# Band attention and a gated network: keys and queries of two heads stacked in the first batch, the global tokens last but one, due times set anew

## The chip, the cores and the metric

One core of a Trainium2 chip runs the whole program. The metric is device time in microseconds (us); the time before is 898.46 us, the median of three runs (897.37 to 899.85). Engine names: PE is the matrix engine (PEld its weight loads), DVE the vector engine, ACT the scalar engine, POOL the general engine, SP the engine whose queue issues every DMA here.

## What is computed

Eight batches of eight heads; 512 local and 32 global tokens a head, head size 64. A local token attends to the 32 global keys and to the local keys at most 32 positions away; a global token attends to all 544 keys. The outputs, 544 tokens of 8 x 64 = 512 values a batch, go through a network with a product gate.

```python
k_all = np.concatenate([k_g, k_l], axis=2)
s_g = scale * np.matmul(q_g, k_all.transpose(0, 1, 3, 2))          # global queries, all keys
s_ll = np.where(np.abs(pos[:, None] - pos[None, :]) <= 32, scale * q_l @ k_l.T, -1e9)
a_l = sm(np.concatenate([scale * q_l @ k_g.T, s_ll], axis=-1))     # local queries
attn = np.concatenate([sm(s_g) @ v_all, a_l @ v_all], axis=2)
h = (x @ w1) * (x @ w2) @ w3                                       # x: attn as 4352 rows of 512
return h @ w_out
```

## The kernel before

Every product is made of float32r parts: an operand is split in a high part (a cast, `hi_of`, mostly on ACT) and a low part (the difference, `lo_of`, on DVE or POOL), and the products of the parts are summed in PSUM.

**A head.** `load_k` brings the keys of one head twice, into the upper and the lower 64 partitions of `kr` (608 columns: local keys with the global ones copied between the blocks). `prep_k` splits them into `kh` and `kl`, `prep_q` puts the high part of the queries in partitions 0 to 63 of `qs` and the low part in 64 to 127. So one matmul over 128 rows multiplies both parts of the queries by `kh`, a second one by `kl`: `scores` issues 2 for each of 4 query blocks, 8 a head. Then follow the row maximum (`mmax`, DVE), the exponentials (`exps`, ACT), seven transposes (PE), the split of the transposed weights (`hi` and `lo`, seven pieces each, tiles PTh, PTl and G), the products with the values (`av`, PE), and a sum of two halves (`cb` on ACT, `sum` on DVE). Two heads make a pair: `join`, `mul` (normalize) and the split of the result into `x` (`xh`, `xl`).

**Global queries.** For each pair of heads `load_kp` brings the keys a second time, as 128 x 544 with one head in either half of the partitions; `prep_kp` splits them (`kph`, `kpl`), and `g_scores` multiplies them by `QG`, 4 matmuls of 272 columns.

**Weights.** In the first 130 us or so 32 packed pieces of the weights (512 KB each) are fetched and unpacked (`unit`: a shift and a merge on DVE, a scaling on ACT). Pieces w3 and wo are multiplied into one matrix (`fold`, 64 steps on PE, tile w34); pieces w12 are split into tiles `W12`, which the last stage uses. All `W12` tiles 0 to 3 are allocated at the start.

**The network.** A quarter of a block of 256 tokens is `first` (tiles ap, bp), a gate (`ga`, `gb`, `gh`, `gl`) and `second` (tile acc). 17 blocks: 16 of local tokens (two a batch) and one of the 256 global tokens of all batches, which comes last. `evict` and `store` write a block in two parts; local tokens go to 128 rows that follow each other (L600), global tokens to 4 places of 32 rows (L602).

**The order** is not the program's text but a list: `list_schedule` simulates five engines with the costs in `COST` and takes on each engine, among the steps whose inputs are there, the one whose due time is earliest. Due times are worked out from the head's number and shifted by the tables `DUE`, `HEADS`, `UNITS` and `SUMS`. `HOLD_A`, `HOLD_D` and `HOLD_H` (ns) are how long a step that two engines can do is kept from one of them: with `HOLD_D` DVE takes a step that POOL can do, with `HOLD_H` DVE takes the cast of a PSUM tile that ACT can do. `LATE` is a penalty in PE's choice.

Of the kernel before, what the change touches and what calls it, by code (L numbers as in the profile page):

```python
# [7 lines left out]
F32 = mybir.dt.float32  # L8
# [22 lines left out]
def i(ap):  # L31
# [12 lines left out]
    w12l=((691, 1300), (420, 752)), w34h=587, w34l=681, scores=897, transposes=690, values=560, gscores=505,  # L44
    gtrans=465, first=1440, second=1405, fold=900,
# [3 lines left out]
MARGIN, LATE, MAIN = 600, 6.0, 2.5e5  # L49
# [6 lines left out]
HOLD_A, HOLD_D, HOLD_P, HOLD_H = 0.1, 0, 90000, 2000  # L56
# [14 lines left out]
    av=(0, -8.3, -53.5, 0), cb=(0, -42.6, 22.6, 0), cg=(-24.3, 42.6, 2.5, 0), clear=(36.2, 0, 0, 0),  # L71
    eg=(11.2, -14.5, 60.9, 0), exps=(-77.6, 1.9, 61.5, 0), fetch=(-6.1, 67.6, -28.7, 0), first0=(0, 0, -0.5, 0),
    first1=(0, 0, 14.2, 0), fold=(0, 82.7, 0, 0), ga=(0, 0, 19.2, 0), gb=(0, 0, -4.6, 0), gh=(0, 0, -57.6, 0),
    gl=(0, 0, -25.9, 0), gw=(0, 35.2, 8.4, 0), hi0=(0, 9.7, -58.6, 0), hi1=(0, -25.8, -77.7, 0),
    hi2=(0, -54.5, -10.4, 0), hi3=(0, -77.2, -22, 0), hi4=(0, -21.9, 24.2, 0), hi5=(0, -3.2, -31.3, 0),
    hi6=(0, 14, 6.1, 0), inv=(-41, -86.6, -72.2, 0), invi=(-2.4, 7.2, -63.4, 0), invo=(-5.2, -59.2, 61.1, 0),
    join=(0, -72, 8.5, 0), joing=(0, 41.8, -10.6, 0), kh=(-29, -66.2, 23.9, 0), kl=(25, -37.7, 45.9, 0),
    kph=(-76.1, 18.5, 3.8, 0), kpl=(22.5, 58.7, 76.8, 0), lcs=(-13.6, 0, 0, 0), lk=(10.3, -26.8, -37.4, 0),
    lkp=(6.7, -0.4, 59.5, 0), lo0=(0, -27.3, -31.1, 0), lo1=(0, -41.7, -128.1, 0), lo2=(0, -80.3, -32.8, 0),
    lo3=(0, -22.1, -19.6, 0), lo4=(0, -11.9, 72.6, 0), lo5=(0, 15.6, 35.1, 0), lo6=(0, -109, -94.1, 0),  # L80
    lq=(9.1, -81.9, -50.8, 0), lqg=(34.3, 46.7, 4.5, 0), lv=(22.9, 41.7, 72.5, 0), lvg=(-24.1, 73.7, -106.8, 0),
    mg=(11.1, 4.8, 28.3, 0), mmax=(-67.6, -19.9, 10.3, 0), mul=(0, 2.8, -12.7, 0), ng=(-9.8, -40.4, 19.2, 0),
    out=(0, 0, 31.5, 0), qgh=(-9.8, 6, 147.2, 0), qgl=(36.9, -10.2, 1.5, 0), qh=(54.2, -4.8, 102.4, 0),
    ql=(-40, 112.7, 18.6, 0), s=(173.8, 31.8, -49.9, 0), second=(0, 0, -11.5, 0), sg=(-103.1, 12.4, -39.4, 0),
    store=(0, 0, 68.3, 0), sum=(0, -31.9, 18.7, 0), t=(0, -40.4, -94.3, 0), tg=(0, -106.1, 15.3, 0),
# [17 lines left out]
}  # L103
SUMS = (-30.2, -40.9, -14, 28.4, 21.4, -13.3, 36.6, 38.3)
# [81 lines left out]
def band_attention_glu_kernel(  # L186
# [120 lines left out]

    def prep_k(n, part, eng=None):
        if part == 0:
            T["kh", n] = p1.tile([128, KD], F32R, tag="kh", name=f"kh{n}")  # L310
            hi_of(T["kh", n], T["kr", n], eng)
        else:
            T["kl", n] = p1.tile([128, KD], F32R, tag="kl", name=f"kl{n}")
            lo_of(T["kl", n], T.pop(("kr", n)), T["kh", n], eng)

    def prep_q(n, part, eng=None):
        if part == 0:
            T["qs", n] = p1.tile([128, 512], F32R, tag="qs", name=f"qs{n}")
# [27 lines left out]
    def scores(n):  # L346
        qs, kh, kl = T.pop(("qs", n)), T.pop(("kh", n)), T.pop(("kl", n))
# [3 lines left out]
        T["sm", n] = p2.tile([128, 4], F32, tag="sm", name=f"sm{n}", bufs=4)  # L351
        for e in range(4):
# [124 lines left out]
    def g_scores(m):  # L477
        kph, kpl = T.pop(("kph", m)), T.pop(("kpl", m))
        sg = ps_1.tile([128, 2, 512], F32, tag="s", name=f"sg{m}")
        for j, kk in enumerate((kph, kpl)):  # L480
# [3 lines left out]
        T["sg", m] = sg  # L484
# [136 lines left out]
    def open_early():  # L621
        P["w12a"] = ctx.enter_context(tc.tile_pool(name="w12a", bufs=1))
        for m in range(MA):
            alloc_w12("w12a", m)
# [141 lines left out]
    def tile_orders():  # L766
        for k in (("k", 0), ("kp", 0), ("kp", 1), ("k", 1)):
            take("kr", NK, (*k, "r"), ("load", *k))
        for k in (("q", 0), ("q", 1), ("vg", 0)):
            take("qr", 3, (*k, "r"), ("load", *k))  # L770
# [4 lines left out]
        for n in range(NH):  # L775
            if n + 2 < NH:
# [22 lines left out]
    def head(n):  # L799
# [3 lines left out]
        add(("load", "k", n), dma(2), t - 12, (), load_k, n, nbytes=2 * 64 * KD * 4)  # L803
        add(("load", "q", n), dma(1), t - 12.1, (), load_q, n, nbytes=64 * 512 * 4)
        for c, tag, due, fn in (("k", "kr", t - 2.0, prep_k), ("q", "qr", t - 1.2, prep_q)):
            h, l = (c + "h", n), (c + "l", n)
            add(h, hi(COST[c + "h"], 600 if c == "k" else 512), due, [("load", c, n)], fn, n, 0, eng=True)
            add(l, either(c + "l"), due + 1.4, [h], fn, n, 1, eng=True)
            read(h, (c, n, "r"))
            read(l, (c, n, "r"), h)  # L810
            read(("s", n), h)
        read(("s", n), ("kl", n))
        add(("s", n), only("PE", COST["scores"]), t + 2.7, [("kl", n), ("ql", n)], scores, n)
# [76 lines left out]
    def global_pair(m):  # L890
# [3 lines left out]
        take("kph", 1, ("kph", m), ("kph", m))  # L894
        take("kpl", 1, ("kpl", m), ("kpl", m))
        add(("load", "kp", m), dma(1), t - 6.0, (), load_kp, m, nbytes=128 * S * 4)
        add(("kph", m), hi(COST["kph"], S), t + 2.3, [("load", "kp", m)], prep_kp, m, 0, eng=True)
        add(("kpl", m), either("kpl"), t + 4.0, [("kph", m)], prep_kp, m, 1, eng=True)
# [251 lines left out]
```

## Time and profile before

| | |
|---|---|
| median of the runs | 898.46 us |
| the profiled execution | 898.57 us, its span 896.8 us |
| PE busy | 844.0 us (94%), 6016 matmuls |
| DVE, ACT, POOL busy | 631.9, 631.4, 424.1 us |
| DMA | 87.06 MB, mean 97 GB/s |
| granted PE clock, mean | 0.983 of full speed |

A profile has a page with busy times, and views that can be cut to an engine, a line or a stretch of time: busy time by stretch, groups of instructions by line, waits (who waited for whom), instructions in order of time. The time above the span (1.8 us) is what lies around the first and the last instruction. The lines that the prediction reads are in a section below.

### The profile page before, as it was taken

The page shows a single profiled execution, that of the slowest core. Times are in us where ns is not written, and L with a number is a line of the kernel's source. Part 1 is how long each engine was busy: PE and PEld are TensorE (multiplying, and loading weights), DVE is VectorE, ACT ScalarE, POOL GpSimd, SP SyncE. Part 2 cuts the span into 40 slices and gives each one's busy share as a digit, 9 for nine tenths or more (in the row PEclk, how much of TensorE's full clock was granted, in tenths as well). Part 3 has the DMA queues.
Part 4 walks back from the last instruction along what each step waited for, and adds up shares of the span by engine and source line. Part 5 has one row for each costly group of instructions (what it writes and reads, how often), then busy time and mean ns, then how long its engine had stood idle before and what let it go on. Part 6 is the DMA issues. An engine that isn't in the chain of part 4 may idle for free.

```text
span 896.8 us, 17972 instructions
## 1 busy us (share of the span) xinstructions
PE 844.0 (94%) x6016; PEld 766.0 (85%) x6016; DVE 631.9 (70%) x1644; ACT 631.4 (70%) x1724; POOL 424.1 (47%) x492
## 2 busy tenths in 40 slices
PE   3879969799999999999999999999999999999995
PEld 2545549699899999999999999999999999999994
DVE  4998988778877778777777777777777787512111
ACT  5887887787878787878787878787877777512111
POOL 4454765655655555555555455555555545200000
PEclk9999989999999999999999999999999999999998
DMA  9877545332242423232323332323232311000000
GB/s 273 246 219 215 181 149 139 118 98 83 65 118 69 111 63 115 61 106 68 113 67 106 77 101 80 101 68 114 65 107 65 108 57 48 13 24 24 1 24 24
DMA packets 52853, 87.06 MB, mean 97 GB/s; under 512 B 16024, under 2 KB 17048, under 8 KB 52760
## 3 DMA queue, kind: packets, MB, share of 16 engines
q1 hardware_dynamic: 52760, 85.92, 33.1%
q8 instruction: 47, 0.77, 0.4%
q14 instruction: 46, 0.38, 0.2%
HBM read 76.84 MB, written 9.04 MB: 96 GB/s over the span
## 4 chain that ended last, share of the span: by engine, by line
PE 87%; DVE 4%; ACT 4%; DMA 2%; issue 1%; POOL 1%; SPq 1%; DVEq 0%; ACTq 0%; POOLq 0%
PE ap L555 7%; PE acc L585 7%; PE acc L587 7%; PE bp L555 7%; PE ap L556 7%; PE acc L586 7%; PE ap L557 7%; PE bp L556 7%; PE bp L557 7%; PE s L355 6%; PE av L446 6%; PE w L692 4%; PE t L391 3%; PE t L394 2%; PE av L441 2%; PE sg L482 2%
## 5 line engine op out<-in xcount | busy, mean ns | idle before, releaser
L555 PE MATMUL bp<-x,w12h 128*128 128x256 f32 x544 | 154.8, 285 | 0.8 <-DVE g__1696 L565 0.8
L555 PE MATMUL ap<-x,w12h 128*128 128x256 f32 x544 | 153.7, 283 | 0.0
L556 PE MATMUL ap<-x,w12h 128*128 128x256 f32 x544 | 152.1, 280 | 0.0
L557 PE MATMUL ap<-x,w12l 128*128 128x256 f32 x544 | 151.6, 279 | 0.0
L556 PE MATMUL bp<-x,w12h 128*128 128x256 f32 x544 | 151.2, 278 | 0.0
L557 PE MATMUL bp<-x,w12l 128*128 128x256 f32 x544 | 151.1, 278 | 0.0
L289 POOL TENSOR_TENSOR kl<-kr,kh 128x608 fp32r<-128x608 f32 x62 | 93.5, 1508 | 104.8 <-ACT kh L286 102.0
L363 ACT ACTIVATE P<-P,mn 128x192 f32<-128x192 f32 (+1 forms) x256 | 121.5, 477 | 5.5 <-DVE mn L359 4.8
L460 DVE TENSOR_TENSOR u<-av,cb 64x352 f32<-64x352 f32 x128 | 65.8, 521 | 58.5 <-ACT cb L286 55.8
L555 PEld LDWEIGHTS bp<-x,w12h 128*128 128x128 f32 x544 | 102.5, 188 | 1.9 <-DVE g__1696 L565 0.9
L556 PEld LDWEIGHTS ap<-x,w12h 128*128 128x128 f32 x544 | 103.6, 190 | 0.5
L555 PEld LDWEIGHTS ap<-x,w12h 128*128 128x128 f32 x544 | 103.5, 190 | 0.5
L556 PEld LDWEIGHTS bp<-x,w12h 128*128 128x128 f32 x544 | 102.5, 188 | 1.1
L557 PEld LDWEIGHTS ap<-x,w12l 128*128 128x128 f32 x544 | 103.4, 190 | 0.0
L557 PEld LDWEIGHTS bp<-x,w12l 128*128 128x128 f32 x544 | 102.4, 188 | 0.0
L359 DVE CUSTOM_DVE_ANT_0 P<-s,cs 128x192 f32<-128x192 f32 (+1 forms) x256 | 87.3, 387 | 7.7 <-PE s L355 5.6
L289 DVE TENSOR_TENSOR PTl<-t,PTh 32x96 fp32r<-32x96 f32 (+1 forms) x192 | 76.3, 397 | 19.2 <-ACT PTh L286 14.3
L286 ACT CAST PTh<-t 32x96 fp32r<-32x96 f32 (+1 forms) x190 | 66.5, 350 | 22.9 <-PE t L391 15.5
L286 ACT COPY cb<-av 64x352 f32<-64x352 f32 x128 | 57.0, 446 | 32.4 <-PE av L446 29.3
L355 PE MATMUL s<-kh,qs 128*128 128x192 f32 (+1 forms) x256 | 65.9, 292 | 8.5 <-DVE mg L497 3.3
L692 PE MATMUL w<-wo,w3f 128*128 128x512 f32 x128 | 63.8, 635 | 3.9 <-DVE wo L616 3.8
L446 PE MATMUL av<-PTl,vs 128*128 128x192 f32 (+1 forms) x256 | 64.5, 277 | 0.0
(786 smaller groups left out, 2350.8 us busy)
## 6 DMA issues: line engine op xcount, KB each, us to landing
kr<-in_kd_t_dram SPq DMA_DIRECT2D x128, 152.0 KB, 2.9
raw_w<-in_w_t_dram SPq DMA_DIRECT2D x24, 512.0 KB, 4.3
kpr<-in_kp_t_dram SPq DMA_DIRECT2D x32, 272.0 KB, 2.7
out_dram<-o SPq DMA_DIRECT2D x34, 256.0 KB, 2.2
qr<-in_q_t_dram SPq DMA_DIRECT2D x64, 128.0 KB, 2.7
vr<-in_v_t_dram SPq DMA_DIRECT2D x32, 256.0 KB, 2.7
R<-rd SPq DMA_DIRECT2D x64, 128.0 KB, 3.0
raw_wo<-in_wo_t_dram SPq DMA_DIRECT2D x8, 512.0 KB, 6.4
```

The lines of the kernel that those rows point to most:

```text
L286: (nc.scalar.copy if eng in (None, nc.scalar) else eng.tensor_copy)(dst, src)
L289: (eng or nc.gpsimd).tensor_sub(dst, src, f(hi))
L355: nc.tensor.matmul(st[:, e, 0:w], qs[:, 128 * e : 128 * e + 128], kk[:, o : o + w], start=(j == e % 2 == 0), stop=(j == 1), skip_group_che ...
L359: nc.vector.tensor_tensor_reduce(blk(n, e), T["st", n][:, e, 0 : WIN[e][1]], masks[e], -0.125, 3.0e38, ALU.add, ALU.min, T["mn", n][:, e : ...
L363: nc.scalar.activation(blk(n, e), blk(n, e), AF.Exp, bias=T["mn", n][:, e : e + 1], scale=-1.0, accum_out=T["sm", n][:, e : e + 1])
L446: nc.tensor.matmul(av[:, o : o + c1 - c0], v, pt[:, j, c0:c1], start=False, stop=(j % 2 == y == 1), skip_group_check=True)
L460: nc.vector.tensor_add(T["u", n // 2][r : r + 64, x], T.pop(("av", n, x))[r : r + 64, 0:352], T["cb", n][r : r + 64, x])
L555: nc.tensor.matmul(d, wh[:, k, c, :], x[:, 0, 0:w], start=(k == m % 2 == 0), stop=False, skip_group_check=True)
L556: nc.tensor.matmul(d, wh[:, k, c, :], x[:, 1, 0:w], start=False, stop=False, skip_group_check=True)
L557: nc.tensor.matmul(d, wl[:, k, c, :], x[:, 0, 0:w], start=False, stop=(k == 3), skip_group_check=True)
L585: nc.tensor.matmul(a, gh[:, m % 2, sl], wh, start=(m == 0), stop=False)
L692: nc.tensor.matmul(T["w34", t], T["w3f", t, j // 4][:, j % 4], T["wo"][:, j], start=(j == 0), stop=(j == 7))
```

## The change

In the first batch (heads 0 to 7) the keys of two heads are loaded once, one head in either half of the partitions, and split once; the same for the queries, whose tile `qs` is now 128 partitions with the high and the low part side by side. The four products of the parts can no longer be summed over 128 rows, so `scores` issues 16 matmuls of 64 rows a head instead of 8 of 128. The stacked keys are just what the global queries of the pair need, so for the first four pairs `load_kp` and `prep_kp` go, and `g_scores` reads pieces of `kh` and `kl`: 12 matmuls instead of 4, since the columns lie apart. Four of the stacked key tiles and all the stacked query tiles are placed in the memory of `W12` tiles 1 to 3 (names e..), which therefore can be filled only when the early scores are done (`free`).

The block of global tokens and the last local block change places (`kk`). All due times, `COST` of four entries and `LATE`, `HOLD_A`, `HOLD_D`, `HOLD_H` are new.

```diff
-    gtrans=465, first=1440, second=1405, fold=900,
+    gtrans=465, first=1395, second=1385, fold=900,
-MARGIN, LATE, MAIN = 600, 6.0, 2.5e5
+MARGIN, LATE, MAIN = 600, 3.0, 2.5e5
-HOLD_A, HOLD_D, HOLD_P, HOLD_H = 0.1, 0, 90000, 2000
+HOLD_A, HOLD_D, HOLD_P, HOLD_H = 400, 1500, 90000, 400
...
-    av=(0, -8.3, -53.5, 0), cb=(0, -42.6, 22.6, 0), cg=(-24.3, 42.6, 2.5, 0), clear=(36.2, 0, 0, 0),
+    av=(0, 2.3, 13.1, 0), cb=(0, -40.5, -5.7, 0), cg=(46.3, -55.7, -7.8, 0), clear=(26.7, 0, 0, 0),
...
     def load_k(n):
-        nc.sync.dma_start(kr[0:64], kd_t[b, h])
-        nc.sync.dma_start(kr[64:128], kd_t[b, h])
+        if n < H:
+            nc.sync.dma_start(kr, kd_t[b, h : h + 2].rearrange("h d k -> (h d) k"))
+        else:
+            nc.sync.dma_start(kr[0:64], kd_t[b, h])
+            nc.sync.dma_start(kr[64:128], kd_t[b, h])
...
+    def early_tile(tag):
+
+        return P["w12a"].tile([128, 4, 2, 128], F32R, tag=f"w12{tag}", name=f"e{tag}_").rearrange("p a b c -> p (a b c)")
+
...
-            for j, kk in enumerate((kh, kl)):
-                nc.tensor.matmul(st[:, e, 0:w], qs[:, 128 * e : 128 * e + 128], kk[:, o : o + w],
-                                 start=(j == e % 2 == 0), stop=(j == 1), skip_group_check=True)
+            c = slice(128 * e, 128 * e + 128)
+            for j in range(4 if n < H else 2):
+                q, k = (qs[r : r + 64, j // 2, c], ks[j % 2][r : r + 64]) if n < H else (qs[:, c], ks[j])
+                nc.tensor.matmul(st[:, e, 0:w], q, k[:, o : o + w], start=(j == e % 2 == 0),
+                                 stop=(j == (3 if n < H else 1)), skip_group_check=True)
...
+        if m < NP:
+
+            for j, kk in enumerate((T["kh", 2 * m], T["kl", 2 * m])):
+                for e, c, o, w in ((0, 0, 0, 128), (0, 128, 160, 128), (0, 256, 320, 16),
+                                   (1, 0, 336, 112), (1, 112, 480, 128), (1, 240, 128, 32)):
+                    nc.tensor.matmul(sg[:, e, c : c + w], QG[:, m], kk[:, o : o + w], start=(j == c == 0), stop=(j == 1),
+                                     skip_group_check=True)
+            return
...
-        key, w = (divmod(k, 2), 256) if k < 2 * B else ((B, 0), TG)
+
+        kk = {2 * B: 2 * B - 1, 2 * B - 1: 2 * B}.get(k, k)
+        key, w = (divmod(kk, 2), 256) if kk < 2 * B else ((B, 0), TG)
...
+            if kind == "w12":
+                free = {1: [("s", 2), ("s", 3), ("sg", 1)], 2: [("s", n) for n in range(H)],
+                        3: [("s", 6), ("s", 7), ("sg", 3)]}.get(a, [])
```

What it moves, at the places that matter below. The first operations of ACT, before (kr, qr, kpr are keys, queries and pair keys as loaded, numbered by head or pair; raw_ are packed weights):

```order
L286 CAST QG_79<-qgr0_107 64x4x32
L286 CAST kh0_147<-kr0_112 128x608
L286 CAST kph0_155<-kpr0_116 128x544
L614 ACTIVATE raw_wo0_0_121<-raw_wo0_0_121 128x512
L286 CAST kph1_176<-kpr1_118 128x544
L489 COPY cg0_179<-sg0_166 64x2x272
```

and now (eh1 is the key tile of heads 2 and 3, eh2 and el2 the query tiles of the first two pairs):

```order
L294 CAST QG_79<-qgr0_93 64x4x32 x2
L294 CAST kh0_118<-kr0_95 128x608
L294 CAST eh1__127<-kr2_98 128x608
L294 CAST eh2__154<-qr0_102 128x512
L519 COPY cg0_158<-sg0_137 64x2x272
L644 ACTIVATE raw_w30_0_104<-raw_w30_0_104 128x512
L294 CAST el2__191<-qr2_107 128x512
```

The casts of pair keys are gone, and a key or query cast serves two heads. The scores of head 0 on PE, before:

```order
L692 MATMUL w34_0_185<-wo_95,w3f0_0_135 128x512
L355 MATMUL s0_194<-kh0_147,qs0_139 128x192
L355 MATMUL s0_194<-kl0_157,qs0_139 128x192
L355 MATMUL s0_194<-kh0_147,qs0_139 128x256
L355 MATMUL s0_194<-kl0_157,qs0_139 128x256
```

and now, the last global piece ahead of them:

```order
L508 MATMUL sg0_137<-kl0_123,QG_79 128x32
L378 MATMUL s0_170<-kh0_118,eh2__154 128x192
L378 MATMUL s0_170<-kl0_123,eh2__154 128x192
L378 MATMUL s0_170<-kh0_118,eh2__154 128x192
L378 MATMUL s0_170<-kl0_123,eh2__154 128x192
L378 MATMUL s0_170<-kh0_118,eh2__154 128x256
L378 MATMUL s0_170<-kl0_123,eh2__154 128x256
```

Each block of columns is met four times instead of twice, and two global scores run ahead of the first fold. The end of SP's queue, before:

```order
L600 DMA out_0_dram<-o7_0_128_11295 128x512
L600 DMA out_0_dram<-o7_1_0_11581 128x512
L600 DMA out_0_dram<-o7_1_128_11583 128x512
L602 DMA out_0_dram<-o8_0_0_11802 4x32x512
L602 DMA out_0_dram<-o8_0_128_11804 4x32x512
```

and now:

```order
L630 DMA out_0_dram<-o7_0_128_11300 128x512
L632 DMA out_0_dram<-o8_0_0_11601 4x32x512
L632 DMA out_0_dram<-o8_0_128_11603 4x32x512
L630 DMA out_0_dram<-o7_1_0_11822 128x512
L630 DMA out_0_dram<-o7_1_128_11824 128x512
```

The stores of the global tokens (o8) are no longer the last.

## Rows read from the trace of the kernel before

**Rows 1.** Busy time by stretch: from:to, length, engines (instructions), PE clock, DMA share, GB/s.

```profile
0.00:20.00 20.00, 5.89 (x16) 3.96 (x17) 8.22 (x20) 10.01 (x21) 10.18 (x15) 1.00 0.90 272
20.00:120.00 100.00, 88.64 (x356) 51.81 (x354) 90.11 (x221) 82.09 (x219) 54.16 (x66) 0.97 0.73 215
120.00:185.00 65.00, 48.95 (x325) 45.75 (x326) 53.28 (x135) 50.22 (x140) 42.64 (x51) 0.87 0.40 120
185.00:250.00 65.00, 63.59 (x490) 60.54 (x490) 51.33 (x134) 51.70 (x146) 35.89 (x42) 1.00 0.32 95
250.00:780.00 530.00, 530.00 (x4072) 504.75 (x4070) 407.25 (x1103) 417.34 (x1167) 276.10 (x313) 1.00 0.30 83
```

**Rows 2.** Waits of PE, 0 to 190 us: total us, times, longest.

```profile
PE sg L482 <- ACT kph L286: 10.9, 1, 10.9
PE tg L516 <- DVE mn L359: 6.6, 1, 6.6
```

**Rows 3.** The last stores: wait, issues; landing of ordinary stores; two stretches as in Rows 1.

```profile
SPq L1146 <- DMA out_dram<-o: 7.4, 1, 7.4
886.99 1.34 SPq L602 DMA_DIRECT2D out_dram<-o  x2
DMA to landing us min/median/max: 2.0/2.0/2.1
860.00:861.00 1.00, 1.00 (x11) 1.00 (x10) 0.22 (x1) 0.00 (x0) 0.00 (x0) 1.00 0.88 336
892.00:893.00 1.00, 0.00 (x0) 0.00 (x0) 0.00 (x0) 0.00 (x0) 0.00 (x0) 0.50 0.26 100
```

**Rows 4.** PE in order of time: start, us of the record, instruction.

```profile
75.21 0.28 PE L355 MATMUL s<-kh,qs 128*128 128x192 f32 x1
...
76.13 7.05 PE L692 MATMUL w<-wo,w3f 128*128 128x512 f32 x16
...
145.78 0.41 PE L482 MATMUL sg<-kph,QG 128*128 128x272 f32 x2
...
146.28 0.39 PE L585 MATMUL acc<-w34h,gh__1520 128*128 128x512 f32 x1
...
147.67 0.60 PE L391 MATMUL t<-cs,P 128*128 128x128 f32 x4
148.10 0.49 PE L394 MATMUL t<-cs,P 128*128 128x128 f32 x3
```

**Rows 5.** Groups of ACT by line and shape, 0 to 190 us: count, busy us, mean ns.

```profile
L286 ACT CAST kh<-kr 128x608 fp32r<-128x608 f32 x14 | 9.7, 696 | 4.9 <-PE s L355 3.4 <-POOL PTl L289 0.9 <-issue 0.3
L286 ACT CAST qs<-qr 64x512 fp32r<-64x512 f32 x14 | 8.6, 611 | 1.7 <-PE s L355 1.5
L286 ACT CAST kph<-kpr 128x544 fp32r<-128x544 f32 x9 | 5.8, 639 | 0.0
```

**Rows 6.** The same view of POOL (first row) and of DVE.

```profile
L289 POOL TENSOR_TENSOR kl<-kr,kh 128x608 fp32r<-128x608 f32 x12 | 18.3, 1523 | 26.4 <-ACT kh L286 23.7 <-ACT G L286 2.6
...
L289 DVE TENSOR_TENSOR G<-t,G 32x384 fp32r<-32x384 f32 x12 | 6.7, 560 | 0.2
L385 DVE TENSOR_TENSOR u<-u,R 128x256 f32<-128x256 f32 x4 | 3.9, 964 | 0.0
...
L289 DVE TENSOR_TENSOR kpl<-kpr,kph 128x544 fp32r<-128x544 f32 x2 | 1.6, 803 | 0.1
```

**Rows 7.** Waits of DVE, 0 to 190 us.

```profile
DVE PTl L289 <- ACT PTh L286: 4.8, 6, 1.9
DVE P L359 <- PE s L355: 4.0, 3, 2.4
```

**Rows 8.** PE, then ACT, in order of time: head 9's values, head 7's scores, a w12 cast.

```profile
153.21 0.37 PE L441 MATMUL av<-G,vgs 128*128 128x288 f32 x1 [0.52 <-DVE G L289]
...
103.89 0.65 PE L355 MATMUL s<-kh,qs 128*128 128x192 f32 x1
...
120.61 0.66 ACT L286 CAST w12h<-raw_w 128x512 fp32r<-128x512 f32 x1
```

More of the change, by code (lines that the diff above doesn't have):

```diff
@@ L76 @@
[L76 to L85, printed above, removed]
@@ new lines @@
+    kph=(0, 36.5, 6.9, 0), kpl=(0, 38.8, -19.3, 0), lcs=(-13.5, 0, 0, 0), lk=(-37.1, -11.5, 42.1, 0),
+    lkp=(0, -72.3, 10.8, 0), lo0=(0, -9.8, 21.6, 0), lo1=(0, 9.1, -38.6, 0), lo2=(0, -6.6, 6.7, 0),
+    lo3=(0, -34.3, -21.3, 0), lo4=(0, -42.8, 22.8, 0), lo5=(0, -8.7, -26.1, 0), lo6=(0, 3.2, 40.7, 0),
+    lq=(-21.7, -11.8, -74, 0), lqg=(-48.9, -72.7, 26.4, 0), lv=(-10.2, -42, -3.3, 0), lvg=(-2, -42.2, 0.5, 0),
+    mg=(-3.5, -61.3, 8.1, 0), mmax=(3.3, -32.6, 17.6, 0), mul=(0, 21.7, -9.6, 0), ng=(-64, 4.8, 34.6, 0),
@@ new lines @@
+    out=(0, 0, 69.3, 0), qgh=(-20.1, -18.6, -59.9, 0), qgl=(55.2, 59.4, 10.2, 0), qh=(-58, 16.7, -8, 0),
+    ql=(-98.3, -8.6, -1.1, 0), s=(-7.3, -65.5, 9.2, 0), second=(0, 0, 62.3, 0), sg=(-54.9, 1.8, -0.1, 0),
+    store=(0, 0, 49.4, 0), sum=(0, -47.6, 32.9, 0), t=(0, -0.4, -16.2, 0), tg=(0, -16.3, 7, 0),
+    u0=(-25.7, 9.7, -1.4, 0), u2=(-3.3, 14.2, -26.4, 0), u3=(54.8, -42.2, -36.7, 0), u4=(0, 21.8, -47.7, 0),
+    u5=(0, -12.3, -3.9, 0), vgh=(-65.9, 0, 53.7, 0), vgl=(-17.7, 0, 62.5, 0), vh=(32.5, 9, 19.2, 0),
@@ L622, in open_early @@
         P["w12a"] = ctx.enter_context(tc.tile_pool(name="w12a", bufs=1))
-        for m in range(MA):
-            alloc_w12("w12a", m)
+        alloc_w12("w12a", 0)
         P["early"] = early_stack.enter_context(tc.tile_pool(name="early", bufs=1))
@@ L664, in unit @@
             if step > 3:
+                if a not in W12:
+                    alloc_w12("w12a", a)
                 hi, lo = (w[:, n * e : n * e + n].rearrange("p a b c -> p (a b c)") for w in W12[a])
@@ L794, in tile_orders @@
             for tag in "kh", "kl", "qh":
-                take(tag, 1, (tag, n), (tag, n))
+                if n >= H or n % 2 == 0:
+                    place = tag
+                    if n < H:
+                        place = f"{tag}{n // 2 % 2}" if tag == "qh" else tag if n % 4 == 0 else f"{tag}{n}"
+                    take(place, 1, (tag, n), (tag, n))
     tile_orders()
@@ L802, in head @@
         t = base(n) - 10.0
[L803 to L813, printed above, removed]
+        n0 = n - n % 2 if n < H else n
+        if n == n0:
+            early = n < H
+            g = (n // 2 // 2 - 1) * 4 + 1 + n // 2 % 2
+            tk = min(t, (base(g) if g > 0 else -14.0) + 6.0) if early else t
+            add(("load", "k", n), dma(1 if early else 2), tk - 12, (), load_k, n, nbytes=(1 if early else 2) * 64 * KD * 4 * (1 + early))
+            add(("load", "q", n), dma(1), t - 12.1, (), load_q, n, nbytes=64 * 512 * 4 * (1 + early))
+            for c, due, fn in (("k", tk - 2.0, prep_k), ("q", t - 1.2, prep_q)):
+                h, l = (c + "h", n), (c + "l", n)
+                add(h, hi(COST[c + "h"], 600 if c == "k" else 512), due, [("load", c, n)], fn, n, 0, eng=True)
+                add(l, either(c + "l"), due + 1.4, [h], fn, n, 1, eng=True)
+                read(h, (c, n, "r"))
+                read(l, (c, n, "r"), h)
+        read(("s", n), ("kh", n0), ("kl", n0), ("qh", n0))
+        add(("s", n), only("PE", COST["scores64" if n < H else "scores"]), t + 2.7, [("kl", n0), ("ql", n0)], scores, n)
         for e in range(4):
@@ L893, in global_pair @@
         b = m // NP
[L894 to L898, printed above, removed]
-        read(("kph", m), ("kp", m, "r"))
-        read(("kpl", m), ("kp", m, "r"), ("kph", m))
-        q = [("qgl", b, r) for r in (0, 64)]
-        add(("sg", m), only("PE", COST["gscores"]), t + 9.0, [("kpl", m), *q], g_scores, m)
-        read(("sg", m), ("kph", m), ("kpl", m))
+        q = [("qgl", b, r) for r in (0, 64)]
+        if m < NP:
+            k = ("kh", 2 * m), ("kl", 2 * m)
+        else:
+            k = ("kph", m), ("kpl", m)
+            for x in k:
+                take(x[0], 1, x, x)
+            add(("load", "kp", m), dma(1), t - 6.0, (), load_kp, m, nbytes=128 * S * 4)
+            add(("kph", m), hi(COST["kph"], S), t + 2.3, [("load", "kp", m)], prep_kp, m, 0, eng=True)
+            add(("kpl", m), either("kpl"), t + 4.0, [("kph", m)], prep_kp, m, 1, eng=True)
+            read(("kph", m), ("kp", m, "r"))
+            read(("kpl", m), ("kp", m, "r"), ("kph", m))
+        add(("sg", m), only("PE", COST["gscores"] + 300 * (m < NP)), t + 9.0, [k[1], *q], g_scores, m)
+        read(("sg", m), *k)
         tiles["QG", b].append(("sg", m))
```

70 lines of the change are left out of this document (41 added, 29 removed), and 20 rows, old and new, of the table UNITS.

## The prediction

> **What bounds the kernel now.** The busy time by stretch comes first [rows 1]. From 250 to 780 us PE is busy for all of its 530 us, while DVE and ACT are at 77 and 79% and POOL at 52%: there PE's own work is the time, and what another engine saves is worth nothing. Before 185 us it is otherwise. PE idles there for 14.1 + 11.4 + 16.1 = 41.6 us (length less PE busy, first three rows), DVE is at 90% from 20 to 120 us and at 82% from 120 to 185, ACT at 82 and 77%. The waits of PE [rows 2] name engines, never PE itself: 10.9 us for the first keys and, as the longest later one, 6.6 us behind DVE. So the first 185 us are a stage in which DVE, and ACT close behind it, unpack weights and carry the first heads, and PE waits. Then comes the tail: the last store is issued at about 888 us, and the queue waits 7.4 us for it [rows 3] with no engine at work.
>
> A common mark makes the sum simple. After the values of head 9 both orders hold the same 5467 matmuls, kind by kind, and ahead of them 485 before and 581 now, the difference being the 64 score and 32 global pieces that are added. Before, this mark is reached at 153.2 us [rows 8]. So the end moves by what the mark moves, by what idle PE has behind it (a part of the third stretch's 16.1 us and 1.4 from 185 to 250, [rows 1]), and by the tail.
>
> **Part 1, the tail.** The store of global tokens writes 4 places of 32 rows. While it runs the DMA engines are at 0.26 of their time and move 100 GB/s; while the two ordinary stores of the block before run they are at 0.88 and 336 GB/s [rows 3]. An ordinary store lands 2.0 us after its issue, and here the wait is 7.4 us. Now two ordinary stores come last. The second issue ends at 888.3 (886.99 + 1.34), having begun about 0.67 before (two issues in 1.34); with 2.0 us from its begin it lands at 889.7, some 1.4 to 1.9 us after the issue's end instead of 7.4: **-5.5 us** (between -5 and -6). The slow store now runs beside a whole block of network work, and nobody waits for it. The work of the last two blocks is the same in size (256 columns either way), so the exchange costs nothing else.
>
> The Trainium skill, "DMA: Bandwidth & Descriptors", section "Why a DMA increments its semaphore by 16 and not by 1", has a rule for it: a copy runs on the largest number of engines up to 16 that divides the slowest dimension of both sides. By that rule 4 places of 32 rows get 4 engines and a store of 128 rows gets 16; the share of 0.26 agrees. It speaks against the rival below in which a last store is slow for being last.
>
> **Part 2, ACT, DVE and POOL in the first stage.** Eight casts of keys and eight of queries become four and four, four casts of pair keys go: on ACT 4 x (0.696 + 0.611 + 0.639) = 7.8 us less [rows 5]. The twelve low parts that go with them were mostly POOL's, 1.5 us or a little less each [rows 6], some 16 us, and this makes room there: by `HOLD_D` POOL takes work from DVE, and by `HOLD_H` DVE takes casts from ACT. I counted the instructions of both orders up to the mark. On DVE 17 go (kpl, kl, ql, mul, vg, v and w12 low parts: 0.5 to 1.1 us each, such as 2 x 0.803 and 2 x 0.964, rows 6), about 12.4 us, and 17 smaller ones come (casts and copies out of PSUM, six of the 32x384 form, not over 0.56 each by the subtraction of that form, rows 6), about 8 us: **-4.4 us on the fullest engine**. ACT loses some 20 us of 134 up to its last cast for head 9, since it gives away casts too. POOL stays within 2 us. How much of ACT's 20 us reaches the mark is not shown by a row, only bounded: DVE's waits for ACT in the stage, such as 4.8 us for PTh [rows 7], are of 14 kinds, 4.8 us down to 0.2, and come to about 12 us without the one at the very start; none or most of them can go. I take -1.5, near the lower end, since 9 us of scores go into the same chain (part 3) and DVE also waits for scores, 4.0 us [rows 7]. Together **-6 us** at the mark, with ends of +5 (the first rival) and -16 (4.4 + 12).
>
> **Part 3, PE's added work.** Eight matmuls of scores take 76.13 - 75.21 = 0.92 us [rows 4]; eight more for eight heads, 7.4 us. The four global matmuls take 0.50 us; as twelve they take between that and 12 x 0.11 = 1.3 us, by the 0.43 us of four transposes of 128 columns [rows 4], so 0 to 0.8 us for four pairs each; nearest are the transposes, 2 to 3 us. Sum 7.4 to 10.6, say 10 us. This is work of a stage in which PE idles 41.6 us, and it is **costed at nothing**: the cover is that idle, and if it were gone the price is those 10 us. No row shows a matmul of 64 rows. Its lower bound is the same 0.115 us as one of 128 rows; its upper bound that no two overlap, and then each takes the 0.28 us of its record: 16 x 0.28 = 4.5 us a head against 0.92, 29 us in all. I take the lower one, because a step depends on columns in every form that the rows have.
>
> The Trainium skill, "TensorEngine Tiling (Array Packing)", section "Key Properties", speaks against the change here: to go from 128-row to 64-row tiles and back drains the engine. No run here shows it. By the rows a drain can cost what a record lasts beyond its step, 0.28 - 0.115 = 0.165 us, twice a head for eight heads 2.6 us; under the same idle it would change nothing, without it the sum would be 2.6 us later.
>
> **Part 4, what is lent and what is moved.** `W12` tiles 1 to 3 wait for early scores. Tile 2 waits for the last, head 7's, which begin at 103.9 us, and its first cast was at 120.6 [rows 8]; in the new order of ACT head 7's exponentials also stand ahead of every w12 cast. Cost nothing; the cover is those 15 us. The loads of the first 20 us fill the DMA engines (share 0.90, rows 1); four pair loads of 272 KB and four pairs of 152 KB go, 2.3 MB, at the 215 GB/s that follow 11 us of transfer, but a weight waits for its buffer and so for DVE, so I count nothing beyond part 2. Behind 250 us PE has no idle to lose, and DVE and ACT hand work to POOL, which was at 52%; PE might wait a little for it: 0 to +2 us, taken as nothing.
>
> **Sum.** From the profiled execution, 898.57 us (0.1 over the median): 898.6 - 5.5 - 6 = **887 us**.
>
> **Rivals.**
> - *The first stage gains nothing or loses a few us* (0 to +5): the heads' chain binds instead of the sum of DVE's work. For it: each head's scores take twice as long, and PE stands in the chain of score, maximum, exponential, transpose. Against: two heads are under way at once, and DVE at 90% leaves little room for a chain. 893 to 898 us, chance 0.17.
> - *The first stage gains much more*, over 13 us: ACT's 20 us all count, 879 us or less. Against: DVE still has all but 4.4 us of its work. 0.08.
> - *The tail stays*: the last store is slow because the machine is idle, not for its shape; 898.6 - 6 = 892.6. Against: the two stores of the block before, also back to back. 0.06.
> - *Slower than before*: 64-row matmuls do not overlap. 29 us more on PE eat most of the 41.6 us, and a head's scores of 4.5 us stand in its chain; with half of it on the path, +14.5 at the mark and no gain of part 2: 898.6 - 5.5 + 14.5 = 907.6. It decides from the point where the mark comes 8.2 us late (901.3), about 1 us a head. 0.06.
> - The forecast, 880 to 893, has 0.63.
>
> **How the numbers follow.** About 0.3% is what a measurement of this kernel can tell from no change, here 895.8 to 901.2. Faster: 0.63 + 0.08 + 0.06 and two thirds of the first rival, 0.11: 0.88. Same: the rest of it, 0.06. Slower: 0.06. The range 880 to 895 holds the forecast, the tail's rival and 0.11 of the first: 0.80.
>
> **What would show it.** Tail: SP's last wait under 2.5 us, and about 4 us between the last matmul and the end that were 10. First stage: values of head 9 at about 147 us, PE idle up to there down by 10 us or more and its busy time up by about as much; 16 score matmuls in about 1.8 us. Main stage: PE busy for all of it. It is wrong if score matmuls stand 0.28 us apart, if PE waits for POOL behind 250 us, or if the last store still takes 7 us.

## The result and the profile after

The changed kernel takes 886.75 us (median of 6 runs, 884.90 to 890.43) where the kernel before takes 898.65 beside it: a ratio of 0.9876, 95% interval 0.9851 to 0.9902. The forecast was 887.0, in a range of 880 to 895. The profiled execution took 887.77 us with a span of 885.6, 11.2 us shorter than the span before. In the columns of [rows 1], its stretches are:

```profile
0.00:20.00 20.00, 11.33 (x48) 10.66 (x49) 5.86 (x20) 11.37 (x25) 12.98 (x18) 1.00 0.90 297
20.00:120.00 100.00, 92.02 (x403) 58.66 (x402) 85.32 (x225) 72.32 (x193) 45.49 (x61) 0.93 0.63 183
120.00:185.00 65.00, 56.36 (x369) 48.69 (x368) 56.47 (x135) 50.11 (x137) 50.54 (x62) 0.92 0.44 131
185.00:250.00 65.00, 64.57 (x499) 61.50 (x498) 51.49 (x143) 46.18 (x132) 45.64 (x57) 1.00 0.35 96
250.00:780.00 530.00, 530.00 (x4072) 504.73 (x4072) 381.19 (x1081) 387.01 (x1072) 332.04 (x419) 1.00 0.29 82
```

The reader is to see three things. From 250 to 780 us nothing has changed for PE: 530 of 530 us busy, with the same 4072 records; POOL went from 276 to 332 us and PE does not wait for it. Before 185 us PE idles 8.7 + 8.0 + 8.6 = 25.3 us where it idled 41.6. And it is busy there 16.2 us longer. The long waits of PE up to 190 us answer to [rows 2]; the 6.6 us behind DVE (`tg`) are gone from the head of the list and the first keys come 5.2 us earlier:

```profile
PE sg L508 <- POOL QG L297: 5.7, 1, 5.7
PE av L464 <- ACT w12h L294: 4.8, 1, 4.8
PE w L723 <- DVE wo L646: 3.8, 3, 2.5
```

The tail answers to [rows 3]. SP's last wait (total, times, longest):

```profile
SPq L1195 <- DMA out_dram<-o: 1.5, 2, 0.9
```

Its last two issues in order of time (start, us), and the landing of these two stores (KB each, median us from issue to landing):

```profile
881.98 1.03 SPq L630 DMA_DIRECT2D out_dram<-o  x2
```

```profile
out_dram<-o SPq DMA_DIRECT2D x2, 256.0 KB, 2.0
```

The stretches of one microsecond in which the store of global tokens runs (860:861) and in which the last two run (883:884), in the columns of [rows 1]:

```profile
860.00:861.00 1.00, 1.00 (x10) 0.92 (x9) 0.17 (x1) 0.00 (x0) 0.00 (x0) 1.00 0.26 102
883.00:884.00 1.00, 0.00 (x0) 0.00 (x0) 0.00 (x0) 0.00 (x0) 0.00 (x0) 1.00 0.98 371
```

From the begin of the last issues to the end of the span it was 896.8 - 887.0 = 9.8 us; now it is 885.6 - 882.0 = 3.6. So the tail gives 6.2 of the 11.2 us. The store of global tokens is as slow as it was (0.26, 102 GB/s), beside PE at 1.00 of 1.00 us.

The remaining 5.0 us are in front of the tail. Split at the mark (values of head 9), in the columns of [rows 1], first the kernel before:

```profile
0.00:153.21 153.21, 118.51 (x539) 78.67 (x540) 126.16 (x309) 118.80 (x311) 86.73 (x104) 0.94 0.70 205
153.21:887.00 733.79, 725.44 (x5477) 687.31 (x5477) 505.76 (x1336) 511.97 (x1412) 337.42 (x388) 1.00 0.26 75
```

And the kernel after:

```profile
0.00:150.38 150.38, 132.43 (x636) 92.89 (x636) 119.04 (x309) 107.54 (x281) 83.63 (x107) 0.95 0.64 189
150.38:882.00 731.62, 723.68 (x5478) 685.78 (x5477) 472.86 (x1309) 477.80 (x1307) 422.16 (x525) 0.99 0.27 76
```

PE's idle time up to the mark fell from 34.7 to 17.95 us, by 16.7, and its busy time rose by 13.9; the mark moved by the difference, 2.8 us. That is not yet the effect of the change: the same changed kernel was run again (below), and there the mark came at 146.57 us. What differs is the clock. In the first profile the granted clock is 0.50 from 37 to 46 us, the lower level of 1.2 GHz; in the second it is 1.00 there, the level of 2.4 GHz, after the same 4.1 us of work in the 7 us ahead. The first profile:

```profile
30.00:37.00 7.00, 4.07 (x19) 2.46 (x19) 6.62 (x20) 5.37 (x16) 3.88 (x4) 0.94 0.66 175
37.00:46.00 9.00, 9.00 (x32) 6.83 (x32) 5.47 (x13) 4.41 (x12) 3.91 (x7) 0.50 0.70 191
```

The second, with its stretch up to the mark:

```profile
30.00:37.00 7.00, 4.09 (x22) 2.47 (x21) 6.62 (x20) 5.39 (x16) 3.86 (x4) 1.00 0.66 184
37.00:46.00 9.00, 8.21 (x49) 5.80 (x48) 7.91 (x17) 8.28 (x22) 6.09 (x10) 1.00 0.70 199
0.00:146.57 146.57, 127.52 (x636) 89.02 (x636) 120.84 (x309) 107.38 (x281) 83.85 (x107) 0.99 0.65 195
```

Three profiles with the old first stage have the mark at 153.2, 153.6 and 155.0 us, three with the new one at 150.4, 150.8 and 146.6: on the mean 153.9 and 149.3, so 4.7 us. A part of that is the clock again. At the lower level a matmul lasts about twice as long: the same twelve matmuls of a global score take 2.47 us at 38.6 us in the first profile and 1.28 us at 37.5 us in the second. Ahead of the mark 12.9, 11.6 and 17.4 us of PE's busy time lie at the lower level in the three old profiles, and 13.3, 12.9 and 3.4 in the three new ones. With half of that taken off, the marks differ by about 2.6 us; that is an estimate. Behind the mark the second run of the changed kernel has PE busy for 725.44 us like the kernel before, so the 1.8 us between 725.44 and 723.68 are taken for variation from run to run.

### The profile page after: what moved, and what is told of

It is laid out like the page before. It is cut to its first block, busy times and chain, and to the rows that moved or that the text cites. A ratio compares the mean times of both kernels' runs of the same rounds, so it can differ in the third digit from the quotient of the medians.

```text
span 885.6 us, 18063 instructions
## 1 busy us (share of the span) xinstructions
PE 856.1 (97%) x6112; PEld 778.7 (88%) x6112; DVE 591.9 (67%) x1617; ACT 585.9 (66%) x1588; POOL 505.8 (57%) x631
## 4 chain that ended last, share of the span: by engine, by line
PE 90%; DVE 6%; ACT 1%; DMA 1%; issue 1%; POOL 1%; SPq 0%; DVEq 0%; POOLq 0%; ACTq 0%
PE bp L585 7%; PE acc L615 7%; PE acc L617 7%; PE ap L585 7%; PE s L378 7%; PE bp L587 7%; PE bp L586 7%; PE acc L616 7%; PE ap L586 7%; PE ap L587 7%; PE av L469 6%; PE w L723 5%; PE t L414 3%; PE t L417 2%; PE av L464 2%; PE sg L513 1%
## 5 line engine op out<-in xcount | busy, mean ns | idle before, releaser
L587 PE MATMUL ap<-x,w12l 128*128 128x256 f32 x544 | 150.8, 277 | 0.0
L297 POOL TENSOR_TENSOR kl<-kr,kh 128x608 fp32r<-128x608 f32 x57 | 88.7, 1557 | 74.1 <-ACT kh L294 60.7
L294 ACT CAST PTh<-t 32x96 fp32r<-32x96 f32 (+1 forms) x150 | 54.5, 363 | 49.6 <-PE t L414 38.5
L723 PE MATMUL w<-wo,w3f 128*128 128x512 f32 x128 | 63.6, 633 | 3.9 <-DVE wo L646 3.8
L469 PE MATMUL av<-PTh,vs 128*128 128x192 f32 (+1 forms) x256 | 63.1, 272 | 0.0
L294 ACT COPY cb<-av 64x352 f32<-64x352 f32 x117 | 52.1, 445 | 13.5 <-PE av L469 11.0
```

What stands on the lines that cost most here:

```text
L294: (nc.scalar.copy if eng in (None, nc.scalar) else eng.tensor_copy)(dst, src)
L297: (eng or nc.gpsimd).tensor_sub(dst, src, f(hi))
L469: nc.tensor.matmul(av[:, o : o + c1 - c0], v, pt[:, j, c0:c1], start=False, stop=(j % 2 == y == 1), skip_group_check=True)
L587: nc.tensor.matmul(d, wl[:, k, c, :], x[:, 0, 0:w], start=False, stop=(k == 3), skip_group_check=True)
L723: nc.tensor.matmul(T["w34", t], T["w3f", t, j // 4][:, j % 4], T["wo"][:, j], start=(j == 0), stop=(j == 7))
```

## The experiments

The runs fall into three groups, each with its own runs of the kernel before beside it, at 898.6, 900.3 and 898.9 us; across groups only the ratios are compared.

**Does the exchange of blocks act alone, and do the two halves add up?** To the kernel before:

```
+        kk = {2 * B: 2 * B - 1, 2 * B - 1: 2 * B}.get(k, k)
+        key, w = (divmod(kk, 2), 256) if kk < 2 * B else ((B, 0), TG)
```

> The kernel before with one edit: the block of global tokens is computed last but one, the last ordinary block last. My theory, the shape of the store makes it slow: the last wait of SP falls from 7.4 us to 1.5-2, the span's end comes 3.5-4 us after the last matmul, total 898.6 - 6 = 892 to 893 (ratio 0.993 to the kernel before). Rival, a last store is slow because it is last: total 898 to 899, wait 7 us as before. The first stage is untouched by the edit, so values of head 9 stay at 153 us.

Measured: 893.16 us against 898.61, ratio 0.9944 (0.9928 to 0.9960): -5.5 us. SP's last wait (total, times, longest) fell as expected, and the mark stayed at 153.63:

```profile
SPq L1147 <- DMA out_dram<-o: 1.7, 1, 1.7
```

The other side, the kernel after with these lines taken out:

> The kernel after with the exchange of the last two blocks undone. If the tail and the first stage add up: 886.8 + 6 = 893 us (0.994 to the kernel before), last wait of SP 7 us again, values of head 9 at 150 us as in the kernel after. Rival, the gain of the tail leaned on the new due times or on the shorter first stage: another difference than that of the run with the exchange alone, by more than 2 us.

Measured: 894.08 us, ratio 0.9953 (0.9938 to 0.9969). 9.6 us from the begin of the last issues to the end of the span, as before; mark at 150.80. The first stage alone gives 4.5 us here, and 6.4 as the difference between the run with the exchange alone and the kernel after (893.16 - 886.75; the kernel before stood at 898.61 and 898.65 beside them); the exchange gives 5.5 and 7.3. Within the intervals the two add up.

**Is the last store slow for its shape or for being last?** The kernel before, where it stays last, with four stores of 32 rows in place of one over four places:

```
-            nc.sync.dma_start(out.rearrange("(b s) c -> b s c", s=S)[t // 32 : (t + tw) // 32, 0:32], o[0:tw])
+            for b in range(t // 32, (t + tw) // 32):
+                nc.sync.dma_start(out[b * S : b * S + 32], o[32 * b - t : 32 * b - t + 32])
```

> The kernel before, in its order, with each of the two last stores (4 places of 32 rows) issued as four stores of 32 rows, eight issues of 0.67 us each in place of two. My theory, a store over 4 places is slow by its shape, and one of 32 whole rows isn't, though it stands last: the eighth issue begins at 887 + 7 x 0.67 = 891.7 and lands 2.0 us later, the last wait of SP falls from 7.4 to under 2 us, the span ends at 893.5 to 894.5, total 2.5 to 3 us less than the kernel before. Rival, whatever is stored last is slow: the eight take 7 us from the last issue, total 3 us or more above the kernel before.

Measured: 895.12 us against 898.93, ratio 0.9964 (0.9950 to 0.9977), 3.8 us by the medians. SP's last wait:

```profile
SPq L1147 <- DMA out_dram<-o: 1.2, 1, 1.2
```

The eight issues in order of time, and their landing:

```profile
888.53 3.62 SPq L603 DMA_DIRECT2D out_dram<-o  x8
```

```profile
out_dram<-o SPq DMA_DIRECT2D x8, 64.0 KB, 1.7
```

The eight issues took 0.45 us each and not 0.67, so the store is ready sooner than expected. So a store is not slow for standing last: the shape is shown to be the cause.

The Trainium skill, "DMA: Bandwidth & Descriptors", section "Why a DMA increments its semaphore by 16 and not by 1", names the slowest dimension as what sets the number of engines. This run agrees: the same bytes with 32 rows as the slowest dimension wait 1.2 us and not 7.4.

**Is it the structure or the due times?** Two crossings: the kernel after with all tuning numbers of the kernel before, and the kernel before with the exchange and all new numbers. In short:

```
-MARGIN, LATE, MAIN = 600, 3.0, 2.5e5
+MARGIN, LATE, MAIN = 600, 6.0, 2.5e5
-HOLD_A, HOLD_D, HOLD_P, HOLD_H = 400, 1500, 90000, 400
+HOLD_A, HOLD_D, HOLD_P, HOLD_H = 0.1, 0, 90000, 2000
...
```

> The kernel after with all of the old tuning numbers of the planner (due times, holds, LATE, and the costs of the two network steps); stacked heads and exchange stay. My theory, the removed casts and low parts carry the gain of the first stage: total 886 to 890, values of head 9 at 152 us or earlier, PE idle to there under 24 us (34.7 before, 18.0 after). Rival, the new times carry it and the structure nothing: 892 to 896, values of head 9 at 153 us or later, since PE has 10 us more of work.

> The kernel before with the exchange of the last two blocks and all of the new tuning numbers (due times, holds, LATE, network costs), but heads of the first batch singly as before. My theory, the structure carries the first stage: 891 to 894, values of head 9 at 152 us or later. Rival, the new times carry it: 886 to 889, values of head 9 at 150 us.

Measured: 908.23 us (ratio 1.0106, 1.0091 to 1.0122) and 915.61 (1.0192, 1.0174 to 1.0209). Both theories fall: with the exchange in all four, the old structure with old times takes 893.2, the new with new 886.8, and the two mixed ones 908.2 and 915.6. The numbers of either kernel fit only its own structure. The marks, 146.2 and 154.0 us, can't be set beside the others: 481 and 450 records stand ahead of them, and not 636 and 539. With the new numbers on the old structure PE waits 16.8 us in one piece for a weight (total, times, longest), which neither of the two real kernels does:

```profile
PE w L692 <- DVE wo L616: 20.6, 5, 16.8
PE sg L482 <- DVE mn L359: 8.7, 3, 6.3
```

PE's busy time up to the last matmul shows what the mixed ones lack; the kernel before, the kernel after, the stacked structure with the old times, the old structure with the new times:

```profile
0.00:887.00 887.00, 843.95 (x6016) 765.99 (x6016) 631.92 (x1644) 630.78 (x1723) 424.15 (x492) 0.99 0.34 98
0.00:882.02 882.02, 856.13 (x6112) 778.66 (x6112) 591.90 (x1617) 585.34 (x1587) 505.79 (x631) 0.99 0.33 95
0.00:902.95 902.95, 863.18 (x6112) 784.88 (x6112) 631.06 (x1644) 624.78 (x1712) 413.22 (x479) 0.98 0.32 93
0.00:911.76 911.76, 853.20 (x6016) 771.04 (x6016) 601.88 (x1614) 591.95 (x1604) 522.44 (x641) 0.98 0.33 95
```

PE idles 43.1, 25.9, 39.8 and 58.6 us. With the old times the stacked structure does nearly without the gain in idle time, and PE's first wait is as long as in the kernel before:

```profile
PE sg L508 <- ACT kh L294: 11.2, 1, 11.2
```

So neither the structure nor the times alone gives the gain of the first stage; it needs both. How it splits between them has no answer from these runs, and stays open: the change is one piece.

**Which engine binds in the first stage?** Six runs leave the order of the kernel after as it is and add or take work on one engine. First less PE work, the added scores taken out again (`range(2)` for `range(4 if n < H else 2)` in `scores`):

> The kernel after, in its order, but the scores of the first batch take only the high parts of the queries: 8 matmuls of 64 rows a head instead of 16 (the low parts of those queries are left out of the result). It takes 64 x 0.115 = 7.4 us of work from PE before values of head 9. My theory, PE's added work lies under waits for other engines: total within 1.5 us of the kernel after (885.3 to 886.8), and PE idle up to values of head 9 goes up by 6 to 7 us, to about 24 us. Rival, the added work is paid at the mark, since idle up to there is already down from 34.7 to 18.0: total 5 to 7.4 us less, 879.5 to 882, PE idle up to the mark unchanged at 18.

Measured: 885.56 us (five runs, 881.8 to 886.4), ratio 0.9830 (0.9807 to 0.9854), against 0.9876 (0.9851 to 0.9902) and 0.9882 (0.9858 to 0.9905) in the two measurements of the kernel after: 4 to 5 us less, with intervals that just touch. The mark came at 143.55 us, 6.8 before that of the first profile at the same clock of 0.95. PE's busy time up to it fell by 8.6 us, from 132.43, and its idle time barely rose, from 17.95 to 19.75 us (143.55 - 123.80):

```profile
0.00:143.55 143.55, 123.80 (x571) 82.91 (x572) 119.46 (x309) 107.08 (x280) 83.92 (x107) 0.95 0.67 198
```

Then more ACT work, in two places, and more DVE work in the second of them:

```
+            for _ in range(2 if n < H else 1):
                 hi_of(T["kh", n], T["kr", n], eng)
```

> The kernel after, in its order, with the eight casts of the first batch (four of keys, four of queries) issued twice, which gives ACT back 4 x 0.70 + 4 x 0.62 = 5.3 us of what the change took from it. My theory, DVE is the engine that binds and ACT's relief counts little: +0 to +1.5 us (886.8 to 888.3). Rival, ACT's time in the first stage counts in full: +4 to +5.3 us, 891 to 892.

```
-            hi_of(W34[t][0], T["w34", t], eng)
+            for _ in range(2):
+                hi_of(W34[t][0], T["w34", t], eng)
```

> The kernel after, in its order, with the eight casts of the folded weights on ACT issued twice: 8 x 0.59 = 4.7 us more on ACT, between 20 and 120 us. My theory (DVE binds): +0 to +1.5 us, up to 888.3. Rival (ACT binds as much): +4 to +4.7, 891 to 891.5. It is the twin of the run with the low parts of the same weights twice on DVE.

```
-            nc.vector.tensor_sub(W34[t][1], T.pop(("w34", t)), f(W34[t][0]))
+            for _ in range(2):
+                nc.vector.tensor_sub(W34[t][1], T["w34", t], f(W34[t][0]))
```

> The kernel after, in its order, with the eight low parts of the folded weights on DVE computed twice: 8 x 0.69 = 5.5 us more on DVE, between 20 and 120 us, in the same chain as the casts of the twin run. My theory, DVE binds: +3.5 to +5.5 us, 890 to 892, values of head 9 at 154 to 156 us. Rival, neither engine binds but the waits between them: +0 to +1.5 us, as in the twin run.

Measured: 887.60 and 888.35 us with more on ACT, ratios 0.9873 (0.9852 to 0.9893) and 0.9879 (0.9859 to 0.9898); 890.36 with more on DVE, 0.9896 (0.9878 to 0.9913). ACT's 5.3 and 4.7 us cost nothing that can be measured in the time; their marks are 149.89 and 150.54 us, at clocks of 0.98 and 0.97. DVE's 5.5 us move the mark by 4.0 (154.35 against 150.38, clocks 0.96 and 0.95) and the time by 1 to 2 us by the ratios, whose interval reaches from nothing to 4: between the two theories. By the medians it is about 2 us more than ACT's, but the intervals overlap.

The last group put the kernel after beside its variants once more:

> The kernel after, unchanged, on the chip of this group, so that the runs beside it are compared with it directly: 0.985 to 0.990 of the kernel before, as measured (886.8 us where the kernel before took 898.6).

Measured: 887.31 us against 898.93, ratio 0.9882 (0.9858 to 0.9905). Beside it, less PE work (`range(3 if n < H else 2)`, so the product of two low parts goes) and more PE work outside the heads:

> The kernel after, in its order, with 12 score matmuls a head in the first batch instead of 16: the product of the low part of the queries with the low part of the keys is left out there. 32 matmuls of 64 rows fewer, 32 x 0.115 = 3.7 us of PE. My theory now, PE is bound by its own work from 60 to 135 us (busy 75 of 75 us) and the added scores are paid: 2.8 (the six heads in that stretch) to 3.7 us less than the kernel after beside it, values of head 9 at about 147 us. Rival, my prediction's view that they lie under waits: within 1 us of it, values of head 9 at 150.

```
-        nc.tensor.matmul(T["w34", t], ..., start=(j == 0), stop=(j == 7))
+        for r in range(3 if j == 0 else 1):
+            nc.tensor.matmul(T["w34", t], ..., start=(j == 0), stop=(j == 7 or (j == 0 and r < 2)))
```

> The kernel after, in its order, with the first matmul of each of the eight weight folds issued three times: 16 x 0.44 = 7.0 us more on PE, none of it in the chain of a head. Two folds begin before 35 us, six between 60 and 115 us, so 12 x 0.44 = 5.3 us of it lies in the stretch that is full. My theory, PE's own work binds there: +4.5 to +7 us against the kernel after beside it, values of head 9 at 155 to 157 us. Rival, it is the length of the heads' chain (score, maximum, exponential, transpose) that binds, and the gain of the run with half the scores came from shorter steps of that chain: 0 to +1.5 us.

Measured: 884.73 us with three products, 2.6 us below the kernel after beside it, all four runs (882.3 to 885.3) below all six of it (885.4 to 889.1), though the two intervals of the ratio overlap (0.9844, 0.9819 to 0.9869). The mark does not tell: it came at 146.45 us at a clock of 0.97, against 146.57 at 0.99 and 150.38 at 0.95 with all four products. And 900.22 with the folds repeated, 12.9 us above. I had sized the dose wrong: each fold stands in the trace as two records (L723 x128 for 64 folds), so that 16 folds are 32 records 0.43 us apart, 13.8 us and not 7.0. The row of the folds on the page of this run (count, busy us and mean ns):

```profile
L724 PE MATMUL w<-wo,w3f 128*128 128x512 f32 x160 | 79.4, 640 | 2.2 <-DVE wo L646 2.0
```

Its stretch up to the mark:

```profile
0.00:164.44 164.44, 147.18 (x668) 99.55 (x668) 121.94 (x309) 107.11 (x281) 82.85 (x107) 0.95 0.56 173
```

The mark moved from 150.38 to 164.44 at the same clock of 0.95, by 14.06 us, all that was added, and PE's idle time up to it is 17.26 us, as much as without it (17.95). None of this work is in a head's chain of score, maximum, exponential and transpose. So it isn't the length of that chain: where the folds stand, PE's own work binds.

## Why the prediction was right, and where it was not

**The tail, right.** Predicted -5.5 (-5 to -6), and 6.2 in the profiles, 5.5 with the exchange alone, 7.3 as what its absence costs. The rival in which a last store is slow for being last is out by the four small stores.

**The sum at the mark, right in its size.** Predicted -6; the profiles give 4.7 on the mean of three each (about 2.6 at a like clock), the runs 4.5 and 6.4. But it came about otherwise than the working says, by two errors against each other, and that they nearly cancel is luck. The sign I named for it did not even fit the sum: idle time down by 10 us and busy time up by as much would leave the mark where it was.

**Part 3 failed: PE's added work is not free.** The size was too small: at like clocks (0.95 and 0.94) PE is busy 13.9 us longer up to the mark, where 10 were predicted. The 9 us more of the second profile (127.5 and 118.5) set a clock of 0.99 against 0.94. A head's scores between two weight folds take 2.53 us from fold to fold where eight took 1.33, so 1.2 more and not 0.92; the twelve pieces of a global score take 1.28 us where four took 0.50; and a head and two of the four global scores stand in the first 20 us, where PE goes at half pace (last section). The cover failed as well. I set the 10 us against the 41.6 us of idle before 185 us, without asking where in that stage the idle lies. Cut finer, the stage shows it. The kernel before, 0 to 60 us, 60 to 120, and 120 to 135:

```profile
0.00:60.00 60.00, 36.18 (x141) 22.55 (x142) 45.34 (x114) 43.30 (x112) 31.11 (x40) 0.95 0.87 254
60.00:120.00 60.00, 58.34 (x230) 33.23 (x228) 52.99 (x126) 48.80 (x127) 33.23 (x40) 0.99 0.66 194
120.00:135.00 15.00, 6.29 (x33) 5.92 (x34) 12.72 (x28) 12.96 (x34) 12.44 (x15) 0.69 0.42 125
```

The kernel after:

```profile
0.00:60.00 60.00, 43.38 (x186) 32.66 (x187) 39.05 (x105) 37.57 (x97) 31.86 (x42) 0.89 0.77 230
60.00:120.00 60.00, 59.97 (x266) 36.66 (x265) 52.13 (x140) 46.12 (x120) 26.61 (x37) 1.00 0.58 174
120.00:135.00 15.00, 15.00 (x86) 10.84 (x84) 13.73 (x34) 12.97 (x35) 13.34 (x17) 1.00 0.43 129
```

Before, PE idles 23.8 us up to 60 us, then 1.7 in the next sixty, then 8.7 in fifteen. The weight folds, 64 of them at 0.86 us between 14 and 120 us, are most of what fills the middle (44.9 of its 58.3 us). The scores of four of the first batch's eight heads stand in that full middle, and there work has no cover, whatever the stage's sum of idle is. Taking the added scores out again takes 8.6 us off PE's busy time up to the mark and adds 1.8 to its idle time, so 1.8 of the 8.6 were covered. In the time it gives 4 to 5 us, taking out half of them gives 2.6 of their 3.7 (32 steps of 0.115), and 13.8 us of folds cost 12.9.

**Part 2 was too small by nearly as much.** Idle time up to the mark went down by 16.7 us (15.7 in the second run). With the added scores taken out it is still down by 15.0 (34.7 to 19.75), so most of it was not filled by them but went for other reasons, and for those I had 6 us. The rows say where: 7.2 us before 60 us, of which 5.2 are the first matmul's start (10.92 before, 5.67 now), and 8.7 between 120 and 135 us, where PE had waited 6.6 us for DVE [rows 2]. I had neither of them in the sum. The early start does not come from the stacked keys alone: with the old times the same structure starts at 11.2 us. DVE's own saving up to the mark is 7.1 and 5.3 us in the two profiles where 4.4 was predicted, POOL's 3.1 where "within 2" was. ACT's is 11.3 us up to the mark; that I gave ACT's relief only 1.5 us was near: 5 us put back on it cost nothing that can be measured in the time. That DVE's relief closed the hole at 120 us is argued from the row that names DVE as what PE waited for, and not shown. The run with DVE's work doubled moves the mark by 4.0 us in one profile, and the time by no more than the noise allows.

**64-row matmuls, right.** They stand as far apart as those of 128 rows, so the rival of 907.6 us is out. In order of time on PE in the kernel after, the first two of a head's sixteen, the last, and the fold behind them:

```profile
84.04 0.35 PE L378 MATMUL s<-eh__273,el__553 64*128 64x192 f32 x1
84.23 0.27 PE L378 MATMUL s<-el__282,el__553 64*128 64x192 f32 x1
...
85.85 0.27 PE L378 MATMUL s<-el__282,el__553 64*128 64x192 f32 x1
86.05 2.84 PE L723 MATMUL w<-wo,w3f 128*128 128x512 f32 x6
```

The first of an eight of 128 rows, and the matmul behind the eight:

```profile
157.10 0.25 PE L378 MATMUL s<-kh,qs 128*128 128x192 f32 x1
...
157.99 0.30 PE L585 MATMUL bp<-x,w12h 128*128 128x256 f32 x1
```

Sixteen take 2.01 us and eight take 0.89, so sixteen at the pace of 128 rows would be 1.78: 0.23 us a head more, which lies at the first step (0.19) and the last (0.20), where most others are 0.11 to 0.14. The step into the group is longer too: the first score begins 0.52 us after the last fold record, and fold records stand 0.43 apart.

The Trainium skill, "TensorEngine Tiling (Array Packing)", section "Key Properties", has a drain at each change between 64 and 128 rows. The trace agrees with such a cost at both ends of the group: about 0.2 us going in and 0.1 coming out, 2.6 us for eight heads if all are like this one, which is the bound in the prediction.

**Part 4 and the main stage, right.** Behind 250 us PE has no wait worth naming, and the lent `w12` tiles held nobody up: the one wait of PE at a `w12h` cast, 4.8 us at 165 us, is for head 10. It ends with a cast of a weight of tiles 4 to 7, while DVE unpacks three such weights one after another ahead of that head's last low part; it is no lent tile coming free.

**What a better working would have been.** Some -16 us of idle time, among it the start and the hole, and +14 of added work, so -2 to -3 at the mark at a like clock, and -6 in the tail: about 890, where 886.75 was measured. The 3 us between are, by the same estimate, the clock (about 2 on the mean of the profiles) and the stretch from the mark to the last stores, 1.3 shorter (732.5 us against 733.8 on the mean of three); why that stretch is shorter stays open. The run with three products at 884.7 us is faster than both kernels, though its result lacks the product of the low parts, and its gain is what the wrong step had called worthless.

## What to carry to other kernels

Idle time covers added work only where the added work stands: cut a stage into stretches short enough that the idle of one is not offered as cover to the work of another, and ask of a "busy" engine in the middle what fills it. A time that comes out right can hide two errors of like size; adding and taking a known dose of work on one engine at a time, in a fixed order, tells which engine binds. Put transfers of a slow shape (here 4 places of 32 rows, at 100 GB/s) ahead of the end, or split them as here into stores of whole rows. Compare a stage's profiles at like clocks only, and don't judge a structure with due times that were fitted to another.

## What the runs showed of the hardware

- The clock was granted differently in two executions of the same program on nearly the same activity: 0.50 and 1.00 from 37 to 46 us, after 4.07 and 4.09 us of PE work in the 7 us ahead, and in the same order of instructions. It moved the mark by 3.8 us and PE's busy time up to it by 4.9 (132.43 and 127.52), so one profile is a poor measure of a stage's gain of 3 us.
- A store of 32 whole rows (64 KB) landed in 1.7 us and its issue took 0.45 us in a row of eight; a store of 128 rows (256 KB) landed in 2.0.
- Each matmul of 512 columns in f32 of the weight fold stands as two records 0.43 us apart: 0.86 us a fold, seen only when a repeat cost twice the expected.
- In the first 20 us PE goes at half of its later pace in both kernels, though the view gives the clock as 1.00 there: the score matmuls of head 0 stand 0.21 us apart, 64 rows or 128, and later ones 0.11 to 0.12. Why is not shown. The kernel after, then the kernel before:

```profile
10.49 0.41 PE L378 MATMUL s<-kl,eh__154 64*128 64x192 f32 x1
10.70 0.41 PE L378 MATMUL s<-kh,eh__154 64*128 64x192 f32 x1
```

```profile
17.01 0.41 PE L355 MATMUL s<-kh,qs 128*128 128x256 f32 x1
17.23 0.41 PE L355 MATMUL s<-kl,qs 128*128 128x256 f32 x1
```
